# A new table of order, raw f32 projections for the first unit, and warming groups in the table, in a fused linear-attention and mixture-of-experts kernel

## The chip, the cores and the metric

One core of one Trainium2 chip. The time is that of the device in microseconds; lower is better. The kernel before took 357.58 us (median of 3 runs, 356.27 to 358.1).

## What is computed

Two stages, one after the other, for 4 batches of 768 tokens.

1. Gated linear attention, 8 heads of 48: for every token `state = alpha_t * state + k_t v_t^T` (alpha scales the rows of the 48x48 state) and `y_t = q_t state`. The heads side by side are `x`, 768 x 384 for each batch.
2. A mixture of 4 attention experts on `x`: for each expert `q, k, v = x @ wq[e], x @ wk[e], x @ wv[e]` (64 wide), causal softmax of `q k^T / 8`, times `v`, times `wo[e]`. Each token takes its best 2 of 4 experts by `x @ w_gate`, with the softmax of the two logits as weights.

All in float32, in and out.

## The kernel before, in words

**Tiling.** The recurrence runs in 24 chunks of 128 tokens (6 for each batch). A chunk has two scans over alpha on VectorE (`sr`, `sc`), products of k and q with them (`mk`, `mq`, on GpSimd but for chunk 0), and on TensorE a transpose of k (`pt`), the products of k with q (`pa`) and of k with v (`pu`), the new state (`ls`, `lm`), and the output (`py`, in two parts). All these TensorE groups consist of many small matmuls: 32 in `pa`, 16 or 32 in `pu`, 80 or 96 in `py` and 16 or 32 in its second part `py.s`, each 48 or 64 rows long.

Three chunks make a unit of 384 tokens; there are 8 units, two for each batch. A unit projects x to queries and keys for two pairs of experts (`pj`), and to values and gate logits (`pv`), then for every pair and each of 3 row blocks: scores (`sc`), maximum and mask (`tt`), exponential (`ex`), normalization and gate (`c0`, `c1`, `nm`), transposes (`tr`), the product with the values (`yv`) and the output projection (`po`), stored by SP.

**Precision.** Operands of projections, scores and outputs are split in two: a rounded high part (type fp32r) and the rest. A product takes three fp32r matmuls: high by high, high by low, low by high. ScalarE writes the high part (`xh`, `wh`, `ph`), VectorE or GpSimd the low one (`xl`, `wl`, `pl`). The weights are loaded once, into tiles that are lent for it (wqk into an `at` tile, wv with the gate into `vg`, wo into `a`), and split once. Transposes, the chunk products and the product with the values use plain f32. For unit 0 (CHUNKED) the projections go in three pieces of 128 columns, one for each chunk, so that a piece can start when its chunk is ready; for other units in one of 384.

**Order.** The program lists 1680 operations (`plan_all`), each with its engine, what it reads and writes and the tiles that it takes. ORDER is a table of their numbers, found ahead of time: the operations are issued in its order, so that it sets the order on every engine and in SP's DMA queue at once. Engines wait for each other by semaphores where an operation reads what another writes, or takes a tile or a PSUM bank that another had. Tiles of a class are handed out in the table's order as they come free: 3 `cr`, 4 `qk`, 4 `v`, 4 `vg`, 7 `a`, 3 `at`. All PSUM work shares 8 banks.

**Start.** Before the table, 26 matmuls of 256 bf16 columns on a constant tile warm TensorE (`warm`, line 449), while the first loads come.

Lines of the profile: 505 `pa`, 516 `pt`, 528 `pu`, 564 and 570 `py`, 601 the state part of `py` and `py.s`, 656 `pj`, 675 `pv`, 725 `sc`, 758 `tr`, 781 `yv`, 802 `po`; 490 and 494 `mk` and `mq`; 646 `wl`.

Of the kernel before, what the change touches and what calls it, by code (L numbers as in the profile page):

```python
# [37 lines left out]
CHUNKED = (0,)  # L38
# [146 lines left out]
def at_off(j):  # L185
# [8 lines left out]


def plan_unit(pl, E, u):
    op = pl.op
    b, hf = divmod(u, 2)
    X = ("x", u)
# [148 lines left out]


def plan_all(E):  # L350
    pl = Plan()
    plan_chunk(pl, E, 0)
    plan_chunk(pl, E, 1)
    plan_weights(pl, E)
# [615 lines left out]
```

## Time and profile before

| | |
|---|---|
| Median of 3 runs | 357.58 us (356.27 to 358.1) |
| The profiled execution: its own time | 353.08 us |
| its span, first to last instruction | 351.3 us |
| mean granted clock of TensorE | 0.956 |
| busy: TensorE, its weight loads | 317.0 us, 269.9 us |
| busy: VectorE, ScalarE, GpSimd | 223.3, 209.6, 193.7 us |
| DMA | 30.22 MB, 28.4% of 16 engines |

The profile is one execution. PE is TensorE's matmuls, PEld its weight loads, DVE VectorE, ACT ScalarE, POOL GpSimd, SP the engine that issues the DMAs. Matmuls overlap in the pipeline, so a mean duration is longer than the pace. A wait is put down to the operation that released it; "issue" means that the profile shows nothing for which the engine waited. PEclk is the granted clock of TensorE as a share of 2.4 GHz; it has two levels, 1.2 and 2.4 GHz.

### The profile page before, as it was taken

How to read it: one execution, taken by the hardware profiler on the slowest of the kernel's cores; microseconds unless marked ns; L12 is line 12 of the kernel's file. 1: busy time of each engine (PE TensorE's matmuls, PEld its weight loads, DVE VectorE, ACT ScalarE, POOL GpSimd, SP SyncE). 2: the span in 40 equal slices, each digit the busy share in tenths (PEclk: the TensorE clock that was granted, in tenths of full speed). 3: DMA queues.
4: the chain of work that ended last, by engine and by line, in shares of the span. 5: the costliest groups of instructions: out<-in, count | busy, mean ns of one | idle time of the engine just before them, and what ended most of it. 6: DMA issues, size and time to landing. Idle time of an engine off the chain costs nothing.

```text
span 351.3 us, 14667 instructions
## 1 busy us (share of the span) xinstructions
PE 317.0 (90%) x6304; PEld 269.9 (77%) x6304; DVE 223.3 (64%) x610; ACT 209.6 (60%) x551; POOL 193.7 (55%) x272
## 2 busy tenths in 40 slices
PE   6649996979989999999998988989999899899993
PEld 4539985869779777888896876878787788797882
DVE  6747984847856684668698595647786385246510
ACT  1415375624766777546786665663866357668971
POOL 5637766818166675592579744943485536024530
PEclk9667999878999999999999999999999999999998
DMA  7965413320236104142171412342160000100111
GB/s 195 299 158 164 134 31 118 87 77 2 81 111 190 27 3 132 56 132 79 41 209 28 135 51 83 107 134 82 42 220 4 4 3 2 49 26 0 50 42 56
DMA packets 13817, 30.22 MB, mean 86 GB/s; under 512 B 1616, under 2 KB 4912, under 8 KB 13744
## 3 DMA queue, kind: packets, MB, share of 16 engines
q1 hardware_dynamic: 13744, 29.21, 28.4%
q8 instruction: 51, 0.84, 1.0%
q14 instruction: 22, 0.18, 0.2%
HBM read 24.48 MB, written 4.72 MB: 83 GB/s over the span
## 4 chain that ended last, share of the span: by engine, by line
PE 76%; issue 7%; DVE 6%; POOL 3%; ACT 2%; DMA 2%; SPq 1%; POOLq 0%; ACTq 0%; DVEq 0%
PE ps L656 14%; PE ps L781 9%; PE ps L758 9%; PE ps L725 9%; PE ps L802 7%; PE ps L675 7%; PE ps L601 5%; PE ps L505 4%; PE ps L528 4%; PE ps L516 3%; PE ps L570 3%; PE ps L564 3%; DMA qk<-in_qk_dram 2%; POOL qk L490 2%; DVE cr L472 2%
## 5 line engine op out<-in xcount | busy, mean ns | idle before, releaser
L754 POOL TENSOR_SCALAR a<-a,cft,gwt 128x640 f32<-128x640 f32 (+5 forms) x96 | 78.4, 825 | 34.1 <-DVE cft L750 26.8
L742 ACT ACTIVATE a<-a,mxt 128x128 f32<-128x128 f32 (+5 forms) x96 | 63.4, 664 | 12.0 <-DVE mxt L736 11.1
L656 PE MATMUL ps<-x,wqk 128*128 128x384 f32 (+1 forms) x360 | 63.4, 328 | 0.0
L769 ACT ACTIVATE at<-ps 128x512 f32<-128x512 f32 (+3 forms) x128 | 52.4, 455 | 16.5 <-PE ps L758 16.2
L736 DVE CUSTOM_DVE_ANT_0 a<-ps,cm 128x384 f32<-128x384 f32 (+3 forms) x96 | 46.5, 504 | 17.9 <-PE ps L725 8.5
L656 PEld LDWEIGHTS ps<-x,wqk 128*128 128x128 f32 x360 | 56.1, 193 | 1.3 <-DVE mxt L736 0.5
L758 PE MATMUL ps<-ident,a 128*128 128x128 f32 x336 | 49.2, 279 | 1.6 <-POOL a L754 1.2
L548 POOL TENSOR_TENSOR st<-ss,cr 112x192 f32<-112x192 f32 x40 | 26.8, 671 | 37.6 <-DVE ss L544 23.9
L758 PEld LDWEIGHTS ps<-ident,a 128*128 128x128 f32 x336 | 39.0, 142 | 6.5 <-issue 2.0
L781 PE MATMUL ps<-at,vg 128*64 128x384 f32 (+2 forms) x324 | 40.5, 393 | 2.0 <-issue 1.0
L490 POOL TENSOR_TENSOR qk<-qk,cr 112x512 f32<-112x512 f32 x23 | 33.0, 1436 | 13.3 <-DVE qk L494 4.4
L725 PE MATMUL ps<-k,q 64*128 64x384 f32 (+3 forms) x384 | 39.2, 337 | 0.0
L472 DVE TENSOR_TENSOR_SCAN cr<-cr,d1r 112x520 f32<-112x520 f32 (+1 forms) x25 | 36.9, 1475 | 3.2 <-DMA cr<-in_al_dram 3.2
L781 PEld LDWEIGHTS ps<-at,vg 128*64 128x64 f32 x324 | 21.1, 136 | 19.7 <-issue 15.1
L483 DVE TENSOR_TENSOR_SCAN cr<-cr,d 112x520 f32<-112x520 f32 (+1 forms) x25 | 35.9, 1444 | 0.1
L748 POOL TENSOR_SCALAR cft<-smt 128x2 f32<-128x2 f32 x48 | 11.4, 236 | 44.5 <-ACT a L742 42.4
L725 PEld LDWEIGHTS ps<-k,q 64*128 64x128 f32 x384 | 29.5, 187 | 5.6 <-issue 1.8
L601 PE MATMUL ps<-qk,st 48*32 48x64 f32 x1408 | 27.0, 232 | 6.7 <-issue 6.3
L675 PE MATMUL ps<-wv,x 128*128 128x260 f32 x216 | 32.6, 298 | 0.0
L494 POOL TENSOR_TENSOR qk<-qk,cr 112x512 f32<-112x512 f32 x23 | 28.2, 1230 | 5.2 <-DVE cr L483 3.6
L802 PE MATMUL ps<-wo,y 128*128 128x384 f32 x144 | 30.3, 349 | 0.0
L675 PEld LDWEIGHTS ps<-wv,x 128*128 128x128 f32 x216 | 28.9, 197 | 0.4
(82 smaller groups left out, 478.0 us busy)
## 6 DMA issues: line engine op xcount, KB each, us to landing
qk<-in_qk_dram SPq DMA_DIRECT2D x23, 448.0 KB, 4.2
v<-in_v_dram SPq DMA_DIRECT2D x24, 256.0 KB, 4.6
cr<-in_al_dram SPq DMA_DIRECT2D x23, 227.9 KB, 4.0
out_dram<-ot SPq DMA_DIRECT2D x24, 192.0 KB, 2.9
at<-in_wqk_dram SPq DMA_DIRECT2D x1, 768.0 KB, 10.3
qk<-in_qk_dram SPq DMA_DIRECT2D x2, 224.0 KB, 4.2
vg<-in_wvg_dram SPq DMA_DIRECT2D x1, 390.0 KB, 9.0
a<-in_wo_dram SPq DMA_DIRECT2D x1, 384.0 KB, 4.8
```

Source lines behind the costliest of these rows:

```text
L472: self.V.tensor_tensor_scan(self.r_(n, p0, np)[:, ::-1], al[:, ::-1], self.d1r[0:P, 0:2 * SW * np], 0.0, OP.mult, OP.max)
L601: m = self.PE.matmul(self.p(py, x)[32 * j:32 * j + 32, CS * kk:CS * kk + CS], L[x][r, p, e:e + 32], q[r, p, x], start=False, stop=y == 1 a ...
L656: self.PE.matmul(self.p(pj)[:, c0:c0 + w], self.wqk[wt][:, k, col:col + 128], x[:, k, c0:c0 + w], start=i == 0, stop=i == 8)
L675: self.PE.matmul(self.p(pv)[:, 0:260], x[:, k, C * i:C * i + C], self.wv[w][:, k], start=m == 0, stop=m == 8)
L725: self.PE.matmul(self.p(sc, e)[:, 0:c1 - c0], q[r, x, C * i:C * i + C], k[r, y, c0:c1], start=m == 0, stop=m == 2, tile_position=(64 * e, 0))
L736: self.V.tensor_tensor_reduce(self.t(A)[:, c0:c1], self.p(sc, e)[:, 0:w], self.cm[:, m0:m0 + w], -1.0 / math.sqrt(HD), mx[:, 0:1] if x els ...
L742: self.A.activation(a, a, AF.Exp, bias=self.mxt[:, x, y:y + 1], scale=-1.0, accum_out=self.smt[:, x:x + 1])
L754: self.G.tensor_scalar(a, a, self.cft[:, c:c + 1], self.gwt[:, u, i, g:g + 1], op0=OP.mult, op1=OP.mult)
L758: self.PE.transpose(self.p(tr)[:, C * (j - j0):C * (j - j0) + C], self.t(A)[:, C * j:C * j + C], self.ident)
L769: self.A.activation(dst, src, AF.Copy)
L781: self.PE.matmul(self.p(yv)[64 * e:64 * e + 64, lo:n1], v[:, j % 3, 64 * g:64 * g + 64], at[e][:, at_off(j) + lo:at_off(j) + n1], start=j ...
L802: self.PE.matmul(self.p(po)[:, 0:DM], y[:, C * i:C * i + C], self.wo[w][:, pair], start=m == 0, stop=m == 5)
```

## The change

- ORDER is a new table, of 1685 numbers. The operations and their reads and writes are the same but for what follows; the order differs throughout, on all engines and in SP's queue.
- Unit 0 (RAW in place of CHUNKED) projects in plain f32: from the raw weights, as they were loaded, and from an x that is not split. `xf` writes that x into an `at` tile with one ScalarE copy for each chunk; unit 0's `xl` is gone. 108 + 27 fp32r matmuls become 36 + 9 f32 ones. The weights are still split for the other units, and the raw ones stay in their tiles until unit 0 has read them.
- Eight warming groups, `fill`, of 4 matmuls of 512 bf16 columns each, are operations of the table and take a PSUM bank each. In the new table four stand ahead of `pt.0`, one between `pu.0` and `py.0`, one behind `pv.0.0`, one in unit 3, one behind the last matmul. The 26 matmuls of `warm` stay.

```diff
-CHUNKED = (0,)
+RAW = (0,)
+NFILL = 8
 ORDER = [int(x) for x in """
-0 5 2 6 10 27 1 3 4 7 28 11 30 8 13 62 18 9 31 12 61 29 32 19 15 33 20 21 14 35 40 16 64 37 41 34 36 55 42 17 67 38
+8 10 34 13 18 14 19 20 15 9 11 37 22 38 35 16 21 17 5 3 0 7 39 23 12 26 24 36 40 27 44 28 25 29 42 1 30 47 67 31 68
...
+    for x in range(NFILL):
+        pl.op(("fill", x), "PE", ("fill", 4), lambda x=x: E.fill(x), w=[("fl", x)], new={("fl", x): "p1"})
...
+            if raw:
+                for x in range(3):
+                    op(pj + (x,), "PE", ("pjf", C), lambda x=x, pj=pj, pair=pair, which=which: E.proj_f(u, pair, which, x, pj),
+                       r=xs[x] + [("wr", "qk")], w=[(pj, x)], new={pj: "p1"} if x == 0 else None)
...
+    if n // HALF in RAW:
+        op(("xh", n), "ACT", ("evict", 384), lambda: E.xf(n, py), r=[py], w=[(("xf", 0), (g, "f"))],
+           new={("xf", 0): "at"} if g == 0 else None)
+        return
...
+    def fill(self, x):
+        for _ in range(4):
+            self.PE.matmul(self.p(("fl", x)), self.zb[:, 0:128], self.zb[:, 0:512], start=True, stop=True)
...
+    def proj_f(self, u, pair, which, g, pj):
+        x = self.xf_()
+        w = self.wraw("qk")
+        col = 256 * which + 128 * pair
+        for k in range(3):
+            self.PE.matmul(self.p(pj)[:, C * g:C * g + C], w[:, k, col:col + 128], x[:, k, C * g:C * g + C], start=k == 0, stop=k == 2)
+
+    def vproj_f(self, u, i, pv):
+        x = self.xf_()
+        w = self.wraw("v")
+        for k in range(3):
+            self.PE.matmul(self.p(pv)[:, 0:260], x[:, k, C * i:C * i + C], w[:, k], start=k == 0, stop=k == 2)
```

The two tables begin as follows on TensorE, read through the list of operations (`pj.u.pair.which.chunk`, which 1 is the keys):

```
before: pt.0 pu.0 pt.1 pa.0 pu.1 pa.1 py.0 py.0.s py.1 pt.2 py.1.s pu.2 pa.2 pv.0.0 py.2 pv.0.1 py.2.s pj.0.1.0.0 pj.0.1.1.0 pj.0.1.1.1 ...
after:  fill fill fill fill pt.0 pa.0 pu.0 fill py.0 pt.1 py.0.s pa.1 pu.1 pv.0.0 fill py.1 pt.2 pa.2 pu.2 py.1.s pj.0.0.1.0 pj.0.0.0.0 pv.0.1 py.2 ...
```

## Rows read from the trace of the kernel before

**Rows 1.** The page's first part: busy us (share of the span) x instructions.

```profile
PE 317.0 (90%) x6304; PEld 269.9 (77%) x6304; DVE 223.3 (64%) x610; ACT 209.6 (60%) x551; POOL 193.7 (55%) x272
```

**Rows 2.** Waits of TensorE: engine line <- releaser: us in total, times, longest.

```profile
PE ps L601 <- issue: 6.3, 7, 1.7
PE ps L570 <- issue: 5.6, 3, 4.7
PE ps L505 <- issue: 2.8, 2, 1.6
PE ps L528 <- issue: 2.5, 2, 1.6
PE ps L516 <- POOL qk L490: 2.3, 1, 2.3
PE ps L564 <- issue: 1.8, 1, 1.8
...
PE ps L781 <- issue: 1.0, 1, 1.0
```

**Rows 3.** Timeline of TensorE: start us, us, what, xcount [wait before <-releaser].

```profile
11.89 1.01 PE L516 MATMUL ps<-ident,qk 112*128 112x112 f32 x4 [2.31 <-POOL qk L490]
...
21.62 0.32 PE L570 MATMUL ps<-ms,v 64*32 64x64 f32 x3 [4.70 <-issue]
...
55.64 0.43 PE L601 MATMUL ps<-qk,st 48*32 48x64 f32 x24 [1.40 <-issue]
...
56.00 0.33 PE L758 MATMUL ps<-ident,a 128*128 128x128 f32 x1
...
59.60 0.61 PE L528 MATMUL ps<-v,kt 64*64 64x48 f32 x16 [1.62 <-issue]
...
67.08 1.51 PE L781 MATMUL ps<-at,vg 128*64 128x384 f32 x12
```

**Rows 4.** Windows from restart to restart: start:end us, busy us (xcount) by engine, clock, DMA.

```profile
55.60:59.50 3.90, 2.34 (x127) 1.95 (x127) 2.12 (x6) 2.69 (x9) 2.56 (x4) 1.00 0.54 148
...
101.10:104.90 3.80, 3.18 (x127) 2.79 (x128) 1.30 (x2) 1.58 (x6) 3.32 (x4) 1.00 0.03 7
```

**Rows 5.** The DMA queues: packets, MB, share of 16 engines.

```profile
q8 instruction: 51, 0.84, 1.0%
```

**Rows 6.** Chain of work that ended last: start us, us, what.

```profile
39.12 7.99 PE ps L656 x72
...
72.59 0.62 PE ps L505 x32
...
81.86 1.08 PE ps L675 x9
...
130.55 3.38 PE ps L781 x24
...
148.50 1.45 PE ps L781 x12
...
154.20 1.56 PE ps L656 x9
```

**Rows 7.** Windows by stage, with the granted clock (PEclk) and the DMA share.

```profile
0.00:20.00 20.00, 11.77 (x221) 9.02 (x221) 13.70 (x23) 5.55 (x8) 12.20 (x29) 0.83 0.92 245
20.00:30.50 10.50, 8.25 (x240) 6.97 (x241) 3.71 (x8) 4.34 (x9) 3.54 (x4) 0.51 0.50 140
...
61.20:64.60 3.40, 3.40 (x18) 3.07 (x18) 2.76 (x9) 1.40 (x5) 2.72 (x4) 0.50 0.70 199
...
74.90:81.70 6.80, 5.96 (x120) 5.53 (x121) 3.84 (x7) 0.58 (x2) 1.93 (x2) 0.50 0.18 62
81.70:351.30 269.60, 251.16 (x4695) 212.92 (x4694) 167.26 (x501) 176.84 (x468) 145.19 (x204) 0.99 0.24 71
```

**Rows 8.** Groups by line and form: shapes xcount | busy us, mean ns | idle before.

```profile
L449 PE MATMUL ps<-d1r 128*128 128x256 bf16 x26 | 5.5, 406 | 1.5 <-POOL d1r L425 1.5
...
L646 POOL TENSOR_TENSOR wqk<-at,wqk 128x768 fp32r<-128x768 f32 x2 | 3.7, 1858 | 0.0
```

More of the change, by code (lines that the diff above doesn't have):

```diff
@@ L193, with plan_unit @@
         ("DVE", ("small", 3), "", ("mx",), "mx"), ("POOL", ("small", 12), "", ("mx", "w"), "w"))
-def plan_unit(pl, E, u):
+def plan_unit(pl, E, u, raw=()):
     op = pl.op
@@ L199, in plan_unit @@
     X = ("x", u)
-    xs = [[(X, (g, z)) for z in "hl"] for g in range(3)]
+    raw = u in raw
+    xs = [[(("xf", u), (g, "f"))] if raw else [(X, (g, z)) for z in "hl"] for g in range(3)]
     for pair in (0, 1):
@@ L203, in plan_unit @@
             pj = ("pj", u, pair, which)
-            gs = [(128 * g, 128, xs[g]) for g in range(3)] if u in CHUNKED else [(0, W3, xs[0] + xs[1] + xs[2])]
-            for x, (c0, w, rs) in enumerate(gs):
-                op(pj + (x,), "PE", ("pj", w), lambda c0=c0, w=w, pj=pj, pair=pair, which=which: E.proj(u, pair, which, c0, w, pj),
-                   r=rs + [("w", "qk")], w=[(pj, x)], new={pj: "p1"} if x == 0 else None)
+            if raw:
+                for x in range(3):
+                    op(pj + (x,), "PE", ("pjf", C), lambda x=x, pj=pj, pair=pair, which=which: E.proj_f(u, pair, which, x, pj),
+                       r=xs[x] + [("wr", "qk")], w=[(pj, x)], new={pj: "p1"} if x == 0 else None)
+            else:
+                op(pj + (0,), "PE", ("pj", W3), lambda pj=pj, pair=pair, which=which: E.proj(u, pair, which, pj),
+                   r=xs[0] + xs[1] + xs[2] + [("w", "qk")], w=[pj], new={pj: "p1"})
             kb = ("k", b, pair) if which else ("q", u, pair)
@@ L217, in plan_unit @@
                 pv = ("pv", u, i)
-                op(pv + ("m",), "PE", ("pv", 260), lambda i=i, pv=pv: E.vproj(u, i, pv), r=xs[i] + [("w", "v")], w=[pv], new={pv: "p1"})
+                fn = (E.vproj_f if raw else E.vproj) if E else None
+                op(pv + ("m",), "PE", ("pvf" if raw else "pv", 260), lambda i=i, pv=pv, fn=fn: fn(u, i, pv),
+                   r=xs[i] + [("wr" if raw else "w", "v")], w=[pv], new={pv: "p1"})
                 op(pv + ("e",), "ACT", ("evict", 260), lambda i=i, pv=pv: E.vevict(u, i, pv), r=[pv], w=[(VG, i)],
@@ L359, in plan_all @@
                 plan_chunk(pl, E, n)
-        plan_unit(pl, E, u)
+        plan_unit(pl, E, u, RAW)
     plan_guard(pl, E)
@@ L621, in xh, with xf, xf_ @@
         self.A.activation(self.xg(n, 0), self.py_(py), AF.Copy)
+    def xf(self, n, py):
+        g = n % HALF
+        self.A.activation(self.xf_()[:, :, C * g:C * g + C].rearrange("p k (s t) -> p s k t", s=2), self.py_(py), AF.Copy)
+    def xf_(self):
+        return self.t(("xf", 0))[:, 0:3 * W3].rearrange("p (k t) -> p k t", k=3)
     def xl(self, n, py):
@@ L631, in load_w, with wraw @@
         self.SY.dma_start(self.t(R)[:, 0:a * w].rearrange("p (a w) -> p a w", a=a), d)
+    def wraw(self, z):
+        a, w = {"qk": self.wqk, "v": self.wv, "o": self.wo}[z][0].shape[1:]
+        return self.t(("wr", z))[:, 0:a * w].rearrange("p (a w) -> p a w", a=a)
     def wparts(self, z, x, R):
@@ L635, in wparts @@
         a, w = hi.shape[1:]
-        raw = self.t(R)[:, 0:a * w].rearrange("p (a w) -> p a w", a=a)
+        raw = self.wraw(z)
         c = slice(256 * x, 256 * x + 256) if z == "qk" else slice(0, w)
@@ L646, in split_wl, with proj @@
         self.G.tensor_tensor(l, w, h.bitcast(F32), OP.subtract)
-    def proj(self, u, pair, which, c0, w, pj):
+    def proj_f(self, u, pair, which, g, pj):
[9 more added lines that the diff above has]
+            self.PE.matmul(self.p(pv)[:, 0:260], x[:, k, C * i:C * i + C], w[:, k], start=k == 0, stop=k == 2)
+    def proj(self, u, pair, which, pj):
         xh, xl = self.x_(u)
@@ L655, in proj @@
             for wt, x in ((0, xh), (0, xl), (1, xh)):
-                self.PE.matmul(self.p(pj)[:, c0:c0 + w], self.wqk[wt][:, k, col:col + 128], x[:, k, c0:c0 + w], start=i == 0, stop=i == 8)
+                self.PE.matmul(self.p(pj)[:, 0:W3], self.wqk[wt][:, k, col:col + 128], x[:, k], start=i == 0, stop=i == 8)
                 i += 1
```

126 rows, old and new, of the table ORDER are left out of this document.

## The prediction, made before the change was run

> **What bounds the kernel now.** I read the page's first part first: TensorE is busy for 90% of the span, no other engine for more than 64% [rows 1]. So the time is TensorE's work, plus what keeps it waiting, plus what it loses at the lower clock level. The waits of TensorE alone come next: seven rows make 22.3 us, and 20.0 of these (6.3 + 5.6 + 2.8 + 2.5 + 1.8 + 1.0, 16 waits) are put down to "issue", that is to nothing that the profile shows; an engine stands behind the one row of 2.3 us [rows 2]. What is "issue" here? The timeline of TensorE shows these waits in the middle of groups whose operands are ready, in groups of many small matmuls [rows 3]. The windows from just before one restart to just before the next give the answer: each holds 127 or 128 matmuls and as many weight loads, 254 or 255 instructions [rows 4] (I looked at four such windows, all with 127 or 128 pairs). Restarts that follow each other lie 3.96 us apart (55.64 and 59.60, [rows 3]); the closest that I found were 3.83 us apart, at 101.17 and 105.00, the stretch of the second window of [rows 4]. The DMA view has a queue for instructions that moved 0.84 MB in 51 packets [rows 5]: 16.4 KB each, and 51 packets for TensorE's 12,608 matmuls and weight loads are 247 to a packet, 256 with the semaphore instructions of its queue and the blocks at either end. So I read "issue" as TensorE waiting for its next block of code, which comes at most every 3.83 us. 32 small matmuls take 0.62 us [rows 6], a block of only these 2.5 us; a block with projections in it (nine in 1.56 us) lasts long enough.
>
> The Trainium skill (Runtime: NRT & Kernel Launch, section Instruction fetch mechanics) says that the code is streamed in 16 KiB blocks of 256 instructions and that crossing a boundary is "mostly hidden". The size agrees with 16.4 KB per packet. "Hidden" does not agree with restarts 128 pairs apart. What follows from "hidden" is a rival below.
>
> The stages show the third term. After 20 us, TensorE is busy for 8.25, 3.40 and 5.96 us at the lower level (clock 0.51, 0.50, 0.50), each time behind an issue wait or a run of small matmuls; from 81.7 us on it stays at the upper one [rows 7]. At the upper level those 17.6 us would be 8.8.
>
> **The change, part by part.**
>
> *The table and the code blocks.* I cut the TensorE column of both tables into pieces of 128 matmuls, set so that the cuts fall where the old waits stand, and added up the work of each piece at full-clock prices. Prices are start-to-start times of the denser quarter of each operation, as in [rows 6]: pa and pu 0.62, py 0.92, its second part 0.39, a value projection 1.08, a projection 1.5, an output 1.0, a product with the values 1.45 or 3.38, a transpose 0.11. The old table has, behind its second cut, 21 of 47 pieces under 3.83 us, together 34.2 us short (the piece "pa.4, py.3, one score" has 1.7 us of work: at its end stands the wait of 1.40 us before 55.64, [rows 3]). The new one has 13, together 9.5 us short; its py and pa groups stand between projections and transposes ("pv.0.2, two scores, two projections, py.3, pt.4": 4.2 us). The old 34.2 us showed as 20.0 - 4.7 = 15.3 us of waits, 0.45 of it, as slow stretches and other waits lengthen the pieces. The same share leaves 4.3 us: **-11.0**. Ends: -15.3, if no piece waits any more, and -6, if blocks arrive later than 3.83 us beside the data transfers.
>
> *The first code wait* (4.70 us at 16.92, [rows 3]) comes in a stage where the DMA engines are 0.92 busy [rows 7]. The loads that stand before it in SP's queue are the same in both tables, but for a later refill of the cr tiles. The fills add 20 matmuls ahead of it, so that its cut moves from py.0 into pa.1 and comes at about 15 us. I take 3.5 us: **-1.2**, between -4.7 and +1.3.
>
> *The lower clock.* Without the waits of 1.4 to 1.9 us between 54 and 76 us I expect no fall there. One stretch remains behind the first code wait, and there the new table has a value projection and a fill in place of 40 more small groups; I take 4.8 us of it, half of it lost: 2.4 against 8.8, **-6.4**, between -8.8 and 0.
>
> *Raw projections.* 108 matmuls of 128 columns go (72 of them take 7.99 us, 0.111 each: the pace of their weight loads, since 384 columns take only 0.173) and 27 of 260 columns (3 x 1.08) [rows 6]. 36 and 9 plain f32 ones come. Plain f32 is in the trace as the product with the values: two records for each matmul, and 6 steps of 2 x 128, 256 and 384 columns, 1536 columns in all, in 1.45 us, 0.94 ns a column [rows 6]; the longer of 3.38 us has 0.88. So 72 records of 128 columns at 0.113 are 8.1 us, and 18 of 260 at 0.229 are 4.1: 12.2 against 15.2, **-3.0**. Ends: -4 where the passes overlap better, and +6.9 where each pass waits for its own weights (72 x 0.222 + 18 x 0.338 = 22.1).
>
> The Trainium skill (FP8 and Floating Point Precision, section TensorE Precision Notes) gives true FP32 four passes. The two records, each at two column times, agree. By passes alone, four would replace the three split products: +1.9 us in place of -3.0. The row decides for -3.0, since the old 128-column matmuls pay for their weights.
>
> *Fills.* 26 warming matmuls of 256 columns take 5.5 us [rows 8], 0.82 ns a column, and half of it at the upper level (384 columns in 0.173 us are 0.45). A fill of 2048 columns costs 0.84 us, or 1.68 at the lower level. Four stand ahead of pt.0 and one ahead of py.0: 4.2 us, in the stretch where the engine now waits three times for VectorE, ScalarE and GpSimd, 3.6 us together, 2.31 of it for the product that pt.1 needs [rows 3]; that work goes on below the fills: +0.6. If that cover were gone they would cost 4.2. Fill 6 comes behind the first code wait, at the lower level: +1.7. Fill 2 lies in the middle of unit 3: +0.84. Fill 4 comes behind the last matmul, beside the last eviction and the last store: nothing. Sum **+3.1**, between 0 and +8.
>
> *The rest.* Unit 0 loses three subtractions on VectorE, which is busy for 64%: nothing. The weights are still split, but for units 1 on. The half of wqk that makes the keys is now split late: GpSimd takes 1.86 us for it [rows 8], behind the chunk products and the first softmax rows in its queue, and between it and unit 1's first projection TensorE has only py.5's second part, one product with the values and one pu group, 0.4 + 1.45 + 0.6 us. That covers it; if GpSimd comes there later, its lateness shows in full. Loads and stores keep number and size. On the way from TensorE through another engine and back, the new table leaves as much TensorE work in between as the old one: **0**, between -3 and +9.
>
> The sum is -11.0 - 1.2 - 6.4 - 3.0 + 3.1 = **-18.5 us** on a span of 351.3, so 332.8. The profiled execution took 353.08 us, 4.5 under the median of the runs (357.58) and 3.2 under the fastest (356.27). I take the difference from the median, and 1 us off it, since the table may place some waits where I see none: 357.6 - 17.5 = **340.1**.
>
> **Rivals.**
> 1. *Other engines' waits take the place.* When TensorE is 5% faster, ScalarE (177 of 269.6 us behind 81.7), VectorE (167) and GpSimd (145) have to be, too [rows 7]. For it: no idle engine is left to hide a late chain. Against it: only 2.3 us of TensorE's named waits are an engine's today. Half of the block and clock gain goes: +8.7, about 349. Chance 0.16.
> 2. *All of it goes*: no code wait behind the first and no low stretch but half of one: -4.3 - 1.2, about 334. Chance 0.08 (beside the forecast's own range).
> 3. *The change does not do what it says.* If crossing a block is hidden, as the page has it, the issue waits have another cause and stay, and with them the low stretches; there remain -1.2 - 3.0 + 3.1: 356.5. Rows 4 speak against it. Chance 0.05.
> 4. *Slower: the at tiles.* There are three. The raw wqk sits in one until its second half is split, the unsplit x of unit 0 in another until the last raw projection; the transposed rows of a pair need two. If the release comes late, evictions of unit 0 wait, PSUM banks stay full and TensorE stops between 45 and 75 us. In the old trace the first pair's transposes and products run from 56.0 to 68.6; both pairs in a row instead of interleaved cost twice 12.6 = 25.2 us: 25.2 - 17.5 = +7.7, 365. It decides from 17.5 us of such waits. Against it: in the new table the last raw projection stands ahead of the first transpose, and the split ahead of pair 1's. Chance 0.08.
>
> **How the numbers follow.** The forecast has 0.63, with 333 to 347 of its own. The range 330 to 353 takes in rivals 1 and 2 and most of what the ends of the terms make, not all ends at once; outside are 3, 4 and a little, some 0.17. A difference of 0.5% (1.8 us) is about what a measurement of this kernel tells from none. Faster by more: 0.63 + 0.16 + 0.08 = 0.87; same 0.05; slower 0.08.
>
> **What would show it.** Right: TensorE's waits for "issue" at 5 to 9 us instead of 20.0, fewer than 8 of them behind the first; a granted clock at the lower level once behind 20 us, and not between 55 and 82; unit 0's projections, 72 and 18 records, at 0.11 and 0.23 us a record; the fourth fill ending near 10 us; TensorE's busy share up from 90% to 93% or more. Wrong: issue waits still 128 pairs apart and above 12 us (rival 3, or blocks that come slower than 3.83 us); long waits of TensorE on ScalarE's evictions into at (rival 4), or many short ones on VectorE and GpSimd (rival 1); f32 records at 0.2 us.

## The result and the profile after

The changed kernel takes 341.58 us (median of 4 runs, 338.7 to 345.15) against 356.92 for the kernel before beside it: 0.9546 of it, interval 0.9463 to 0.9629. The forecast was 340.1, range 330 to 353.

The first profile of the changed kernel is that of its slowest execution (345.15 us), so the rows below are of a second profile of the same kernel (340.62 us, span 338.9), but for one pair of views that is named. Line numbers have moved: 522 `pa`, 533 `pt`, 545 `pu`, 581 and 587 `py`, 618 the state part of `py` and `py.s`, 683 and 689 the raw f32 projections, 697 `pj`, 716 `pv`, 766 `sc`, 799 `tr`, 822 `yv`, 843 `po`, 462 `fill`, 466 `warm`.

The page's first part, as [rows 1]: TensorE is busy for 95% of the span.

```profile
PE 323.2 (95%) x6287; PEld 265.0 (78%) x6291; DVE 214.5 (63%) x607; ACT 207.6 (61%) x551; POOL 183.4 (54%) x272
```

Waits of TensorE, as [rows 2]. "Issue" is 3.4 + 2.6 + 1.6 = 7.6 us in four waits (two more are of 0.3 and 0.2), instead of 20.0 in sixteen; the waits for GpSimd, VectorE and ScalarE before 20 us are gone.

```profile
PE ps L522 <- issue: 3.4, 1, 3.4
PE ps L618 <- issue: 2.6, 2, 1.6
PE ps L587 <- issue: 1.6, 1, 1.6
PE ps L466 <- POOL d1r L438: 1.5, 1, 1.5
PE ps L766 <- DVE k L709: 0.3, 1, 0.3
```

Timeline of TensorE, as [rows 3]: the four code waits, still in the middle of groups, and the first four fills, behind which the chunk products start at 9.92. The window from the second restart to the third, as [rows 4], holds 128 matmuls and 127 weight loads once more.

```profile
6.47 3.62 PE L462 MATMUL ps<-d1r 128*128 128x512 bf16 x16
9.92 0.55 PE L533 MATMUL ps<-ident,qk 112*128 112x112 f32 x4
...
18.28 0.92 PE L522 MATMUL ps<-qk 48*64 48x64 f32 x25 [3.36 <-issue]
...
26.20 0.25 PE L587 MATMUL ps<-ms,v 64*32 64x64 f32 x2 [1.61 <-issue]
...
30.07 0.32 PE L618 MATMUL ps<-qk,st 48*32 48x64 f32 x8 [1.02 <-issue]
...
55.53 0.41 PE L618 MATMUL ps<-qk,st 48*32 48x64 f32 x20 [1.56 <-issue]
```

Windows (start:end, length, busy us (xcount) of PE, PEld, DVE, ACT, POOL, granted clock, DMA share, GB/s), as [rows 4] and [rows 7]. The first is the window between the two restarts. The second and third are the only two stretches at the lower level; from 72 us to the last few microseconds the clock stays up, and TensorE idles for 266.9 - 260.9 = 6.0 us where it had idled for 18.4 [rows 7].

```profile
26.15:30.02 3.87, 2.78 (x128) 2.19 (x127) 1.20 (x4) 1.68 (x4) 0.77 (x2) 1.00 0.02 4
...
16.08:22.90 6.82, 4.62 (x63) 3.72 (x64) 3.16 (x5) 0.00 (x0) 3.49 (x4) 0.50 1.05 266
57.04:60.45 3.41, 3.41 (x23) 3.41 (x17) 2.59 (x8) 1.75 (x6) 0.65 (x1) 0.50 0.46 137
72.00:338.90 266.90, 260.93 (x4876) 214.48 (x4876) 167.00 (x506) 175.63 (x469) 139.37 (x208) 1.00 0.24 71
```

The chain, as [rows 6]: 18 raw f32 records of 128 columns in 2.02 us (0.112 each), 12 in 1.53 where a group of another kind stands beside them (0.128), 6 of 260 columns in 1.51 (0.252).

```profile
34.87 2.02 PE ps L683 x18
...
40.20 1.51 PE ps L689 x6
42.44 1.53 PE ps L683 x12
```

Groups by form, as [rows 8] (xcount | busy us, mean ns | idle before): the fills are 7.0 us of TensorE's time (28 of their 32 records are in the trace).

```profile
L462 PE MATMUL ps<-d1r 128*128 128x512 bf16 x28 | 7.0, 379 | 0.4 <-issue 0.2
```

### The profile page after: what moved, and what is told of

The parts are those of the page before. It is cut to its first block, busy times and chain, and to the rows that moved or that the text cites. A ratio compares the mean times of both kernels' runs of the same rounds, so it can differ in the third digit from the quotient of the medians.

```text
span 343.4 us, 14610 instructions
## 1 busy us (share of the span) xinstructions
PE 326.7 (95%) x6291; PEld 267.9 (78%) x6291; DVE 213.3 (62%) x607; ACT 208.2 (61%) x551; POOL 183.2 (53%) x272
## 4 chain that ended last, share of the span: by engine, by line
PE 91%; issue 3%; DMA 2%; SPq 1%; DVE 1%; ACT 0%; ACTq 0%
PE ps L697 13%; PE ps L799 13%; PE ps L766 12%; PE ps L822 11%; PE ps L843 8%; PE ps L716 7%; PE ps L618 5%; PE ps L522 4%; PE ps L545 4%; PE ps L533 3%; PE ps L683 3%; PE ps L581 3%; PE ps L587 3%; DMA v<-in_v_dram 2%; PE ps L689 2%
## 5 line engine op out<-in xcount | busy, mean ns | idle before, releaser
L795 POOL TENSOR_SCALAR a<-a,cft,gwt 128x512 f32<-128x512 f32 (+5 forms) x96 | 72.8, 767 | 16.2 <-DVE cft L791 12.3
L697 PE MATMUL ps<-x,wqk 128*128 128x384 f32 x252 | 48.5, 341 | 0.0
L766 PE MATMUL ps<-k,q 64*128 64x384 f32 (+3 forms) x384 | 44.0, 346 | 0.3 <-DVE k L709 0.3
L697 PEld LDWEIGHTS ps<-x,wqk 128*128 128x128 f32 x252 | 42.8, 188 | 0.8 <-issue 0.2
L565 POOL TENSOR_TENSOR st<-ss,cr 112x192 f32<-112x192 f32 x40 | 24.4, 609 | 29.6 <-DVE ss L561 24.5
L507 POOL TENSOR_TENSOR qk<-qk,cr 112x512 f32<-112x512 f32 x23 | 27.9, 1219 | 15.1 <-DVE cr L489 8.6
L511 POOL TENSOR_TENSOR qk<-qk,cr 112x512 f32<-112x512 f32 x23 | 30.8, 1340 | 6.9 <-DVE cr L500 6.7
L489 DVE TENSOR_TENSOR_SCAN cr<-cr,d1r 112x520 f32<-112x520 f32 (+1 forms) x25 | 32.6, 1312 | 1.4 <-DMA cr<-in_al_dram 1.4
L500 DVE TENSOR_TENSOR_SCAN cr<-cr,d 112x520 f32<-112x520 f32 (+1 forms) x25 | 32.2, 1294 | 0.2
L716 PE MATMUL ps<-wv,x 128*128 128x260 f32 x189 | 28.2, 298 | 0.0
L514 ACT ACTIVATE junk<-cr 112x1041 bf16<-112x1041 f32 x24 | 25.7, 1071 | 1.3 <-DVE cr L500 1.3
```

What stands on the lines that cost most here:

```text
L489: self.V.tensor_tensor_scan(self.r_(n, p0, np)[:, ::-1], al[:, ::-1], self.d1r[0:P, 0:2 * SW * np], 0.0, OP.mult, OP.max)
L697: self.PE.matmul(self.p(pj)[:, 0:W3], self.wqk[wt][:, k, col:col + 128], x[:, k], start=i == 0, stop=i == 8)
L716: self.PE.matmul(self.p(pv)[:, 0:260], x[:, k, C * i:C * i + C], self.wv[w][:, k], start=m == 0, stop=m == 8)
L766: self.PE.matmul(self.p(sc, e)[:, 0:c1 - c0], q[r, x, C * i:C * i + C], k[r, y, c0:c1], start=m == 0, stop=m == 2, tile_position=(64 * e, 0))
L795: self.G.tensor_scalar(a, a, self.cft[:, c:c + 1], self.gwt[:, u, i, g:g + 1], op0=OP.mult, op1=OP.mult)
```

## The experiments

Theory: TensorE waits wherever 128 pairs of its code take less time than the next block needs to arrive, and the new table puts longer work into these pieces. Rivals: the waits belong to certain operations; or the gain is that of the raw projections or of the warming.

**The changed kernel again (a_same)**, beside the next three:

> The changed kernel itself, once more, as the yardstick for the other runs and for a second profile. Its first profile took 343.4 us of span, above the other three runs (337.0 to 340.7), with three stretches at the lower clock level behind 18 us. Theory (the clock stretches and the first code waits are what differs between its runs): a faster execution has the same work and the same two long code waits in the first 30 us, each within 1 us, but fewer microseconds at the lower level. Rival (the execution differs in waits spread over the whole span): the clock is alike and the waits differ. Time 338 to 343 us.

Measured: 341.11 us (340.62 to 344.28), 0.9655 of before [0.9596, 0.9714]. The rows above are its. Its stretches at the lower level are shorter, as expected (10.2 us against 17.1 in the slowest execution), but the second code wait is not within 1 us of the first profile's: 1.61 instead of 3.56 us, and there is one more of 1.02.

**Is it the block of code? The old table with the cuts elsewhere (b_shift).** The warming of the kernel before is cut into more, smaller matmuls: 64 more pairs in front of an unchanged table.

```diff
-26 warming matmuls of 256 columns
+20 of 256 columns, 70 of 16 columns
```

> The kernel before with its warming matmuls cut differently: 20 of 256 columns and 70 of 16 in place of 26 of 256, 64 matmuls more, about as long in time; its table and all else stay. Theory (TensorE waits for blocks of 256 of its instructions): all waits for issue move by 64 matmuls and weight loads in the stream, so that they again stand 256 instructions apart but at other operations: none in py.3's second part at 54 us, one in py.4, one in py.12 instead of py.11, at the places of the table where the shifted pieces are short (22 pieces under 3.83 us, 38 us short, against 21 and 34): 15 to 20 us of issue waits behind the first, the time within 3 us of before. Rival (the waits belong to operations or to transfers): they stay at the same operations, 54.24, 58.04, 73.89 us and so on.

Measured: 362.84 us, 1.0249 [1.0153, 1.0346]. Waits of TensorE (as above) and its timeline:

```profile
PE ps L601 <- issue: 12.7, 9, 2.4
PE ps L564 <- issue: 4.9, 1, 4.9
...
PE ps L570 <- issue: 3.0, 2, 1.7
PE ps L528 <- issue: 1.6, 1, 1.6
```

```profile
24.97 0.32 PE L564 MATMUL ps<-ms,v 64*32 64x64 f32 x3 [4.95 <-issue]
...
34.26 0.41 PE L601 MATMUL ps<-qk,st 48*32 48x64 f32 x19 [1.29 <-issue]
...
75.83 1.09 PE L528 MATMUL ps<-v,kt 64*64 64x48 f32 x31 [1.59 <-issue]
```

The waits now stand in other operations: `pa` (line 505), which had 2.8 us in two waits [rows 2], has none, and lines 601 and 564 have more. Counted in the records of TensorE's queue (matmuls, weight loads and semaphore instructions), all of them come at the same place modulo 256 (records 705, 1217, 2241, 3265, 4289, ...: 193 and a multiple of 256), as in the kernel before and after. The packets of the instruction queue say the same: all 33 such waits of 0.5 us and more, in the executions of before, of b_shift and the two of the changed kernel, end 1.2 to 1.6 us after the end of a packet of 16,384 bytes. Behind the first they make 17.3 us, where 15.3 stood before. So they belong to the cuts between blocks, not to operations: that is shown. The Trainium skill (Runtime: NRT & Kernel Launch, section Instruction fetch mechanics) calls crossing "mostly hidden"; where the 128 pairs are small matmuls, these runs disagree. The time was missed: not within 3 us of before but 8 over, with more time at the lower level (11.0 to 31.5 us, and four stretches behind it: 32.2 us of TensorE's busy time against 22.6, half of the difference lost).

**Is it the raw projections? The old table with them (b_raw).** Order of before, no fills; unit 0 projects in plain f32 and its `xl` is gone.

```diff
-CHUNKED = (0,)   # split, three pieces of 128 columns
+RAW = (0,)       # plain f32; old order of the operations, NFILL = 0
```

> The kernel before with the raw projections alone: its old table without unit 0's three subtractions, no warming groups in it, unit 0 in plain f32 from raw weights and the unsplit x. Theory (the old table keeps its issue waits; raw saves 3.0 us of TensorE's work, at 34 to 47 us where nothing else holds TensorE): 2 to 4 us faster than before, about 352 us, issue waits of 18 to 21 us. Rival (the raw form gives most of the whole gain, as undoing it cost 9.7 us): 346 us or less.

Measured: 359.03 us (355.72 to 363.75), 1.0141 [1.0034, 1.0249]: not faster, so the theory of this run fell. The waits for "issue":

```profile
PE ps L617 <- issue: 11.1, 8, 2.4
PE ps L586 <- issue: 7.2, 4, 3.7
...
PE ps L521 <- issue: 1.9, 2, 1.4
...
PE ps L580 <- issue: 1.3, 2, 1.1
```

45 fewer matmul records in unit 0 (135 become 45 matmuls of two records) shift every later cut, and the old table, whose pieces are short, waits for 21.5 us instead of 20.0. TensorE is busy for 316.4 us of a span of 353.8, against 317.0 of 351.3: of the 3.0 us of work that were to be saved 2.6 are lost again at the lower level, where 27.7 us of the busy time lie instead of 22.6, and the idle time grew by 3.1 us, half of it code waits.

**And without them? The new table with split projections (a_split with fills, c_table without).**

```diff
-RAW = (0,)
+RAW = ()      # unit 0 split, pieces of 128 columns; xl, wh, wl where unit 0 needs them
```

> The changed kernel with the raw projections undone: unit 0 projects again from split weights and a split x, in pieces of 128 columns, at the same places of the table; the splits of wv and of both halves of wqk and the three subtractions for x are put ahead of it. Theory (the raw form saves 3.0 us of TensorE's work, 12.2 against 15.2 us, and frees the first projections from the splits): 3 to 6 us slower, with 135 matmuls of 0.11 to 0.12 us in place of 90 records. Rival (unit 0's projections lie beside code waits anyway, since 90 more instructions per wait stretch the blocks): within 1.5 us of the changed kernel.

> The new table alone: the split projections of unit 0 in three pieces, as in the kernel before, and no filling groups. If the gains of the parts add up in this table (undoing the raw projections cost 9.7 us, leaving out the fills gave 2.2), it is at 341.1 + 9.7 - 2.2 = 348.6 us, some 7 faster than the kernel before, with under 5 us of issue waits of TensorE behind the first and none of them in the chunk products one after the other. Rival: the table gains only together with the raw projections, as these gained nothing in the old table either; then it is within 2 us of the kernel before.

Measured: a_split 350.84 us, 0.9878 [0.9816, 0.994]; c_table 348.74, 0.9869 [0.9795, 0.9944]. So the table alone brings some 5 us, and the raw projections some 10 in it (a_split 9.7 above a_same), more than the 3 to 6 expected, though they cost time in the old one. The time expected for c_table, 348.6, came; its code waits behind the first are 4.4 + 1.7 = 6.1 us, not under 5. The first part of its page, its waits and its lower stretches:

```profile
PE 326.8 (94%) x6304; PEld 272.1 (78%) x6304; DVE 212.6 (61%) x610; ACT 208.0 (60%) x551; POOL 184.6 (53%) x272
```

```profile
PE ps L619 <- issue: 4.4, 2, 4.0
PE ps L534 <- issue: 2.7, 1, 2.7
PE ps L523 <- issue: 2.2, 1, 2.2
PE ps L588 <- issue: 1.7, 1, 1.7
...
PE ps L767 <- DVE q L710: 1.0, 1, 1.0
```

```profile
8.41:22.06 13.65, 10.73 (x249) 9.08 (x257) 7.80 (x15) 3.86 (x8) 9.05 (x7) 0.50 1.05 266
25.49:39.14 13.65, 12.09 (x241) 10.98 (x242) 4.42 (x7) 2.17 (x5) 7.16 (x6) 0.50 0.33 87
66.45:69.87 3.42, 3.42 (x32) 3.09 (x39) 2.27 (x6) 1.70 (x7) 1.17 (x1) 0.51 0.57 170
```

a_nofill (below) is c_table with raw projections. Counted from the last matmul backwards, the two executions run parallel: c_table is 9.2 us behind at 75 us and stays within 1 us of that to the end. All of it arises before: 3.4 + 6.8 us more at the lower level, half of them lost (5.1), 1.3 more of waits for VectorE and some 1.2 more for code, and the matmuls themselves.

c_table has the same 6304 matmuls as the kernel before, in another order. TensorE's idle time falls from 34.3 us [rows 1] to 20.4, but its busy time rises from 317.0 to 326.8. Of these 9.8 us the lower level explains 1.8 (26.2 us of the busy time instead of 22.6); 8.0 us more go to the same matmuls.

**The fills (a_nofill).** `fill` issues nothing.

```diff
-        for _ in range(4):
-            self.PE.matmul(self.p(("fl", x)), self.zb[:, 0:128], self.zb[:, 0:512], start=True, stop=True)
+        pass
```

> The changed kernel without the eight warming groups; the 26 warming matmuls stay. Theory (the fills cost TensorE 0.84 us each at the upper level; the four in front of pt.0 and the one in front of py.0 lie over waits, fill 6 costs about 1 us, fill 2 0.9 and fill 4 nothing; they do not prevent the stretches at the lower level, which follow the code waits): the kernel gets 1 to 3 us faster, the first code wait stays at 3 to 5 us, and the stretches at the lower level stay within one of their number. Rival (the fills keep the clock up): a longer stretch at the lower level in the first 35 us, and 2 to 5 us slower.

Measured: 338.91 us (337.0 to 339.41), 0.9558 [0.9506, 0.961], 2.2 under a_same. Its lower level:

```profile
8.63:22.28 13.65, 10.85 (x238) 8.80 (x238) 8.96 (x16) 3.69 (x7) 9.45 (x7) 0.50 1.05 272
25.74:32.57 6.83, 5.41 (x119) 4.70 (x119) 2.01 (x5) 2.18 (x5) 1.68 (x3) 0.50 0.20 48
```

The fills do keep the clock up, 10.2 us at the lower level against 20.5 without them, and still cost more than that gives back. The first code wait is 2.0 us here, not 3 to 5.

**The second code wait (a_loads).** In the slowest execution of the changed kernel this wait is 3.56 us, and TensorE had entered the block before it at 18.60: 128 pairs in 5.70 us, longer than the 3.83 that a block needs at best. That row of its waits, and two windows, up to the cut and the wait itself:

```profile
PE ps L587 <- issue: 3.6, 1, 3.6
```

```profile
18.60:24.30 5.70, 5.70 (x127) 4.32 (x127) 3.90 (x4) 1.12 (x2) 3.40 (x3) 0.70 1.06 215
24.30:27.90 3.60, 0.04 (x3) 0.00 (x0) 0.00 (x1) 0.00 (x0) 2.07 (x2) 1.00 0.77 177
```

The DMA engines were full (1.06) with loads issued at 12.55 to 15.88 us. The packet of the next block started at 24.99, 6.4 us after the cut before it; behind the other two waits of this execution, at 27.90 and 59.18, it starts 1.1 and 1.2 us after. So the last two of these loads (`lq.5`, `lw.o`), which stood ahead of a load that is issued only at 31.85 us (`lq.4`), were moved behind it, and the two conversions of wo behind operations of chunks 4 and 5.

```diff
 the order of loads and conversions
-lq.5 ... lw.o ... lq.4 ... wh.o ... ck.4 ... wl.o ... mk.5
+lq.4 lq.5 lw.o ... ck.4 wh.o ... mk.5 wl.o
```

> The changed kernel with two loads put later in SP's queue: the q and k of chunk 5 and wo, 0.83 MB together, issued behind those of chunk 4 (about 32 us instead of 15 us), and the split of wo behind them. Theory (the second code wait, 3.56 us at 24.3 us, is a code block that is held up by data transfers: its block started 6.4 us after TensorE entered the block before, against about 1.2 us later in the trace, while the DMA engines were fully busy): that wait falls below 1.5 us, the stretch at the lower level behind it gets shorter or goes, and the kernel gets 2 to 5 us faster. Rival (blocks come at their own pace whatever the data do): the wait stays at 3 to 4 us and the time within 1 us.

Measured: 339.07 us (338.09 to 342.88), 0.9589 [0.9526, 0.9653], 2.0 under a_same, at the lower end of what was expected (the two sets of runs overlap); the wait at this cut is gone, and so is the lower stretch at 57 us. The packet in question came 6.4 us after the cut in the slowest execution (wait 3.56 us), 5.2 in a_same (1.61) and 2.7 here (none).

```profile
PE ps L521 <- issue: 3.4, 1, 3.4
...
PE ps L617 <- issue: 1.4, 2, 0.8
PE ps L682 <- issue: 0.6, 1, 0.6
```

**What does a change of tile shape cost? (a_sw64, a_sw128).** The account below leaves 8 us of TensorE's time over. In order of the program, neighbouring matmuls of different tile shapes (rows x columns of the array) follow each other 153 times in the old table and 233 times in the new. Both runs add 56 matmuls of 64 columns, two inside each 384-wide projection of units 1 to 7, into columns that nobody reads: a_sw64 on a 64x64 tile, so that the shape changes 112 times more, a_sw128 on the full array.

```diff
+                if i in (3, 6):
+                    self.PE.matmul(self.p(pj)[0:64, 448:512], self.zb[0:64, 0:64], self.zb[0:64, 0:64], start=False, stop=False, tile_position=(0, 0))
```

> The changed kernel with 56 small matmuls added: two in each of the 28 projections of 384 columns, behind the third and the sixth of its nine matmuls, 64 rows by 64 columns of weights and 64 columns wide, into unused columns of the same PSUM bank. Question: why TensorE's work outside the named waits runs slower under the new table. Theory (a change of the tile shape of the array makes TensorE wait until the matmuls in flight are through; in the trace the next weight load starts 0.07 us before the end of the matmul ahead of it where the shape changes, 0.27 to 0.33 us before it where it stays): every added matmul makes two such changes of 0.20 to 0.26 us, 22 to 29 us in all, beside its own 0.03 us: the kernel takes 362 to 372 us. Rival (a change of shape costs nothing; what slows the new table is something else): 56 x 0.03 to 0.11, 2 to 6 us, as with the full shape.

> The same 56 added matmuls, but with the full shape of 128 rows by 128 columns of weights, as the projections around them have, 64 columns wide. Theory (only a change of shape costs): 56 x 0.05 to 0.11 us, 3 to 6 us: 344 to 348 us. Rival (any added matmul costs the same): as much as with the small shape.

Measured: a_sw64 360.55 us, 1.0184 [1.0083, 1.0285]; a_sw128 348.5, 0.9844 [0.975, 0.9937]. 12.0 us for 112 changes are 0.107 us each, about half of the 0.20 to 0.26 expected, while the matmuls themselves cost 7.4 instead of 3 to 6. (Two runs of each; in the profiled executions 10.2 of the difference are TensorE's busy time, 0.09 for a change, and 3.3 are code waits.) The timelines of the same projection in both, a_sw64 first: from one three of line 697 to the next it is 0.87 us (110.69 to 111.56), and 0.67 (107.50 to 108.17) where the shape stays.

```profile
110.69 0.79 PE L697 MATMUL ps<-x,wqk 128*128 128x384 f32 x3
111.41 0.21 PE L700 MATMUL ps<-d1r 64*64 64x64 bf16 x1
111.56 0.79 PE L697 MATMUL ps<-x,wqk 128*128 128x384 f32 x3
```

```profile
107.50 0.79 PE L697 MATMUL ps<-x,wqk 128*128 128x384 f32 x3
108.13 0.20 PE L700 MATMUL ps<-d1r 128*128 128x64 bf16 x1
108.17 0.77 PE L697 MATMUL ps<-x,wqk 128*128 128x384 f32 x3
```

The Trainium skill (TensorEngine Tiling (Array Packing), section Key Properties) says that a change of tiling mode drains TensorE, without a price; these runs agree and give one. In the traces of before and after, behind 72 us and at the upper level, the next weight load starts 0.07 us before the end of the last matmul at each change, and 0.25 to 0.49 us (medians of the five common shapes) before it where the shape stays.

**A better version (c_loads_nofill, c_loads2_nofill, c_loads2).** The moved loads without the fills; the same with the load of wqk behind the fourth load of v too (it is the raw wqk that moves; the expectation calls it the low half); and that one with the fills.

```diff
 a_loads, and in it
-            self.PE.matmul(self.p(("fl", x)), ...)
+        pass
 in the two with loads2, in the order of loads
-lw.qk ... lv.3
+... lv.3 lw.qk
```

> The changed kernel without its filling groups and with the loads of wo and of the sixth q moved behind later loads. If the second code wait came from those loads and the fills only delay, both gains add up: 341.1 - 2.2 - 2.0 = 336.9 us, between 335 and 339, the fastest so far. Rival: without the fills the cuts between the blocks of code lie elsewhere (20 matmuls of fills ahead of the first cut are gone), so a block is again fetched beside other loads; then 339 or more, with an issue wait of over 2 us behind the first.

> As the run before, with the load of the low half of the q and k weights' tile moved behind the fourth v load too, so that the first code wait has fewer transfers beside it. If the first wait is set by the transfers that stand in the DMA engines when its block is asked for, it falls from about 3.4 us towards 1.5 and the time by 1 to 2 us, to some 335.5. Rival: the moved load is then late for the first projection, which takes the gain back: no change or slower by up to 2 us, with a wait of TensorE for SyncE's transfers or the weights near 25 us.

> The same moved loads with the fills kept: tells whether the fills are worth anything once no block is late. Theory: they still cost 1.5 to 3 us, so 337.5 to 339. Rival: with a clock that stays up behind them they gain, 336 or less.

Measured: c_loads_nofill 335.48 us (333.84 to 336.58), 0.9512 [0.9446, 0.9578]; c_loads2_nofill 335.23, 0.9492 [0.9414, 0.9569]; c_loads2 339.13 (337.37 to 341.91), 0.9621 [0.9547, 0.9695]. The first beats both kernels. Its median is also under the 338.91 and 339.07 of its two parts alone, but these are of another set of runs, and by the ratios to the kernel before (0.9512 against 0.9558 and 0.9589) the intervals overlap. Its waits, and its one stretch at the lower level with what follows:

```profile
PE ps L531 <- issue: 2.6, 1, 2.6
PE ps L520 <- issue: 1.9, 1, 1.9
```

```profile
8.30:21.99 13.69, 11.18 (x246) 8.79 (x254) 10.20 (x16) 3.72 (x8) 9.02 (x8) 0.50 0.96 276
22.00:332.60 310.60, 301.49 (x5995) 249.97 (x5995) 201.15 (x583) 202.04 (x541) 169.71 (x243) 0.99 0.28 80
```

The 2.6 us stand ahead of the first transpose, at the place of the fills. The later load of wqk gained nothing: the first code wait was 3.2 us with it and 1.9 without, so the expected 1.5 was wrong, and a load of v came 1.6 us late, much as its rival had it. Waits of c_loads2_nofill:

```profile
PE ps L520 <- issue: 3.2, 1, 3.2
...
PE ps L543 <- DMA v<-in_v_dram: 1.6, 1, 1.6
```

With fills the time is 339.13, without 335.23: they cost 3.9 us, more than in a_nofill and than the 1.5 to 3 expected.

## Why the prediction was right, and where not

The account goes by TensorE's busy and idle time, the profiled execution of before (span 351.3) against a_same's (338.9), a difference of -12.4 where the steps made -18.5.

| step | predicted | measured |
|---|---|---|
| code waits behind the first | 15.3 to 4.3: -11.0 | 1.61 + 1.02 + 1.56 = 4.2: -11.1 |
| first code wait | 4.70 to 3.5: -1.2 | 3.36: -1.3 |
| lower clock | -6.4 | busy there 22.6 to 8.0 us, half lost: -7.3 |
| raw projections | 12.2 for 15.2: -3.0 | 12.6 to 13.7: -1.5 to -2.6 |
| fills | +3.1 | 7.0 us busy, 3.6 of other waits covered: +3.4 |
| changes of tile shape | not in the sum | +8.0 to +9.1, as what is left over |
| TensorE's other waits, most of them for engines | not in the sum | about -2.6 |

*The code blocks.* Right in mechanism: b_shift shows that the waits go with the cuts. Rival 3 falls. That the size came out to 0.1 us is partly luck: the share of short pieces predicted the sum, not the places. 13 pieces were short and three waits came, and the one of 1.61 us at 26.20 is a block held up by data transfers, as a_loads shows, which the prediction had as its lower end ("if blocks arrive later"); without it some 2 us remain (1.4 + 0.6 in a_loads).

*The lower clock.* "One stretch remains, 4.8 us" was right for what lies behind the first code wait (4.62 us busy), but a second came at 57.04, behind the wait before 55.53, where none was expected; and 4.96 us of the kernel before lay at the lower level at 10.02 to 16.85, which the prediction left out. In the slowest execution the changed kernel spends 17.1 us there (at 18.65, 28.89 and 59.61), and by the prediction's count the step gains next to nothing. So its size depends on how late a block comes, and was taken as too certain.

*The missing step.* With these terms TensorE's busy time should be 317.0 + 7.0 - 7.3 less 1.5 to 2.6, so 314.1 to 315.2 us; the page has 323.2. The 8.0 to 9.1 us more are for the same matmuls. c_table, without fills and raw projections, shows 8.0 for the order alone. What costs them is the change of tile shape: the new table has 80 more, and at the 0.107 us of a_sw64 and a_sw128 these are 8.6 us. The traces show it in the kernels' own groups as well. Behind 72 us and at the upper level, the time from the start of a matmul to the start of the next is longer at a change of shape than the mean for its kind, by 0.13 us on average: summed up, 15.3 us for 115 changes in the old table and 23.9 us for 190 in the new, 8.6 more. So the prediction failed in "The rest ... 0", which held that the new order itself costs TensorE nothing: its price for a group was that of the denser quarter, and such groups stand beside their like. The new table takes them apart to lengthen its pieces of code, so the gain in waits was bought with drains. No run keeps the pieces of code and takes the changes away.

*Raw projections.* A record of 128 columns was priced at 0.113 and took 0.112 to 0.128; one of 260 at 0.229 and took 0.252. But that the parts add up was wrong: by the medians b_raw loses some 4 us to before, a_split 10 to a_same. An edit that shifts the cuts has no price of its own; it has one in each order. (The +1.9 us that the prediction works out by passes alone covers, by its size, only the 36 matmuls for queries and keys; the nine of 260 columns would add about 1. Nothing hangs on it.)

*Fills.* Right within a microsecond (+3.4 for +3.1), and a loss in time: 2.2 us by a_nofill, 3.9 by c_loads2.

*Rivals.* 1 did not come: TensorE's longest wait for another engine's work behind 20 us is 0.3. The prediction gave it too little to start from: its list leaves out smaller rows, and behind the warming the waits for other engines were not 2.3 us but 6.8 in the old trace (the largest left out are 1.2 for GpSimd at line 758 and 1.0 for VectorE at line 781). They went all the same. 2 did not come in the changed kernel; c_loads_nofill comes near its time (335.5 for about 334) and has no code wait over 0.7 us behind the first, but 11.2 us of busy time at the lower level. 4 did not come: no wait for an `at` tile is in the list.

*The time.* The median fell by 15.3 us beside the result and by 14.1 in the first set of runs, not by 17.5; 340.1 was 1.5 under. That it came so near is partly luck. Between the profiled executions the sum was 6.1 us too large (18.5 for 12.4): the missing 8 us were made good in part by the waits for engines, and the forecast took 1 us off. The profiled execution of the kernel before was also one of its faster ones (353.08 for a median of 356.92), that of the changed kernel close to its median (340.62 for 341.58), so that the medians lie 2.9 us further apart than the two executions.

## What to carry to other kernels

Where TensorE waits for "issue" in groups of small matmuls, count its records between restarts: if they are 256 every time (128 pairs of weight load and matmul), it is the block of code. Then spread the small groups among long ones, and keep bulk loads out of the transfers at the first cuts. Price a group with its neighbours: each change of tile shape costs 0.09 to 0.13 us here, so interleaving is paid for. Test an edit of the instruction count in the order in which it will run, since every later cut moves with it.

## What the runs showed of the hardware

- TensorE's waits without a named releaser, but for the one ahead of the first transpose where the fills are left out, stand a multiple of 256 records of its queue apart, whatever the operation (b_shift), and end 1.2 to 1.6 us after a code packet of 16,384 bytes has come.
- A block of code waits behind data transfers: its packet started 6.4 us after the cut before it, with the DMA engines at 1.06, instead of 1.1 to 1.2 in the same execution.
- A change of tile shape costs TensorE 0.107 us by a_sw64 and a_sw128, 0.13 us on average in the kernels' own groups; the weights' load of the next matmul starts 0.07 us before the end of the last instead of 0.25 to 0.49.
- A plain f32 matmul on 128 columns is two records of 0.112 us, the time that an fp32r one of 128 columns takes with its weight load (0.111, [rows 6]): two for three.
- Open: what sets the length of the first code wait (1.9 to 4.0 us under the new table, 4.7 and 4.9 under the old), which the moved weight load did not shorten.
